# Two tiles in seven products beside one plain tile in the even batches' last chunks, and smaller moves of copies, mends and a bank

## Chip, cores and metric

The kernel runs on one core of one Trainium2 chip. The metric is the time of one execution on the device in microseconds (us).

## The reference

```python
def reference(x, w_tok1, w_tok2, w_ch1, w_ch2):      # x: 8 x 3008 x 256
    X = np.fft.fft(x, axis=1)
    x = np.fft.fft(X, axis=2).real.astype(np.float32)
    xt = x.transpose(0, 2, 1)
    h = np.maximum(xt @ w_tok1, 0.0) @ w_tok2         # 3008 -> 256 -> 3008
    u = x + h.transpose(0, 2, 1)
    h2 = np.maximum(u @ w_ch1, 0.0) @ w_ch2           # 256 -> 1536 -> 256
    return u + h2
```

A Fourier transform over both axes, then a mixing of tokens and a mixing of channels, each with a relu and a residual.

## The kernel before

The program walks 8 batches of 6 chunks. A chunk is up to four tiles of 128 rows. For each of its 12 steps (`ct`) the first channel product `mm1` makes one slice of the hidden layer (`pc` in PSUM, relu into `c1`), while the *previous* chunk's second channel product runs from its finished `c1`. There are two forms of that second product. The plain one (`mm2`) makes a tile with 12 matmuls of 256 columns. The other (`mm2_seven`) takes tiles in pairs and computes 2 x 2 blocks with seven products for eight, each product of 12 matmuls of 128 columns (two pairs), with sums prepared on VectorE. The last chunk of an even batch has only three whole tiles and a half one, so it was done plainly:

```python
    def seven(b, c):                       # which chunks take the seven products
        if c == NCH - 1:
            return b % 2 == 1 and b < BB - 1
        return b > 0 or c >= 2
# [cut]
    def product(dst, left, right, first):
        for a in range(2):                 # two pairs of tiles
            for k in range(NH):            # NH = 6
                nc.tensor.matmul(dst[:, P * a:P * a + P], lhsT=left[:, k, a, :],
                                 rhs=right[:, k, :], start=(first and k + a == 0),
                                 stop=(k == NH - 1), skip_group_check=True)
# [cut]
    sum_at = {0: 1, 1: 2, 3: 4, 4: 3}      # step: sum made on VectorE
    places = {0: 0, 1: -1, 2: 1, 5: 2, 6: 3, 8: 4, 10: 5, 11: 6}   # step: product
# [cut] for b, for c:
            joins = prev is not None and seven(*prev[0:2])
            on_v = ((1, 5, 8), (), ())[c] if b == 0 and c < 3 else () if joins else (0, 3, 6, 9)
            for ct in range(NCT):          # on_v: relus on VectorE, the others on ScalarE
                mm1(b, c, c1, ct, on_v)
# [cut]
                if joins:
                    if ct in places:
                        mm2_seven(*prev, places[ct], pbox)
                    if ct in sum_at:
                        sums(prev[2], pbox, sum_at[ct])
                elif prev is not None and ct % 3 == 2:
                    mm2(*prev, ct // 3, pbox)
# [cut] at the end of a chunk: the half tile is kept for the next batch
            if c == 5 and b % 2 == 0:
                G.tensor_copy(out=tail1[:], in_=c1[:, :, 384:448])
```

Two PSUM banks serve the results: products 0, 2, 4 and 5 gather in one (`pa`), products 1, 3 and 6 in the other (`pb`), and a plain tile with `ks = 2` (`po`) uses that second bank too.

Before the first channel product there is a set-up of 34 us. VectorE folds the input of batch 0 (`fa`, `fb`, `eo`), TensorE transforms it (`pz`), ScalarE copies the result (`z`), TensorE applies the second-stage table `td` (`pw`), and so on through `ph`, `hq`, `pt`, `uv`, `uu`, `pu`, `ut` to the first `pc`. The table needs three small mends on VectorE (and a memset), and these stood in the middle of the fold. Copies of `hp` and `hq` went by turns to VectorE and ScalarE:

```python
    take(fold0, 5)                                   # first half of the fold
    ts(ol[:, 0:1], ol[:, 0:1], 2.0, AT.mult)         # the mends
    ts(td[:, 0:1], td[:, 64:65], 0.5, AT.mult, ol[:, 0:1], AT.add)
    ts(td[:, 65:66], td[:, 64:65], 0.5, AT.mult, ol[:, 0:1], AT.subtract)
    V.memset(td[:, 64:65], 0.0)
    take(fold0, 5)                                   # second half
# [cut]
                copy(g2 % 2, dst[:, 2 * g2:2 * g2 + 2, :].rearrange("p g k -> p (g k)"),
                     ph[:])                          # true: VectorE, false: ScalarE
# [cut]
                pt = ps_f("pt1")
```

## Time and profile before

| | before |
|---|---|
| time, median of 3 runs | 600.62 us (600.14 to 601.08) |
| span in the trace | 598.5 us |
| first `pc` | 34.19 us after the start |
| from first `pc` to the end | 564.3 us |
| TensorE busy | 582.7 us, 97% of the span |

A row of a timeline reads: start in us, duration, engine, line of the program, operation, output <- inputs, sizes, number of instructions joined in the row, and in brackets the idle time of the engine just before with what ended it. Durations of joined rows contain the end of the last instruction. For a rate one takes start to next start.

The split at the first `pc` is the one used throughout: what is before is called set-up, what is after the steady part. A set-up gain is a shorter chain; in the steady part TensorE has hardly any gaps, so a gain there is TensorE time taken away.

### The profile page before, as it was taken

The page shows a single profiled execution, that of the slowest core. Times are in us where ns is not written, and L with a number is a line of the kernel's source. Part 1 is how long each engine was busy: PE and PEld are TensorE (multiplying, and loading weights), DVE is VectorE, ACT ScalarE, POOL GpSimd, SP SyncE. Part 2 cuts the span into 40 slices and gives each one's busy share as a digit, 9 for nine tenths or more (in the row PEclk, how much of TensorE's full clock was granted, in tenths as well). Part 3 has the DMA queues.
Part 4 walks back from the last instruction along what each step waited for, and adds up shares of the span by engine and source line. Part 5 has one row for each costly group of instructions (what it writes and reads, how often), then busy time and mean ns, then how long its engine had stood idle before and what let it go on. Part 6 is the DMA issues. An engine that isn't in the chain of part 4 may idle for free.

```text
span 598.5 us, 15332 instructions
## 1 busy us (share of the span) xinstructions
PE 582.7 (97%) x6273; PEld 418.5 (70%) x6273; DVE 445.2 (74%) x917; ACT 393.9 (66%) x760; POOL 255.3 (43%) x396
## 2 busy tenths in 40 slices
PE   3999999999999999999999999999999999999997
PEld 3756676677767776677767777667776777666776
DVE  8779679675898669766897668856688657966663
ACT  8856764477647865577756866558665876546662
POOL 8650655837554654635348445556555000000000
PEclk9999999999999999999999999999999999999999
DMA  8993912376127814494335632376123422324533
GB/s 155 206 187 72 181 37 60 72 141 109 46 63 133 137 41 69 77 177 54 78 76 100 131 84 55 67 157 104 41 60 79 90 55 55 81 58 78 92 73 88
DMA packets 83415, 55.70 MB, mean 93 GB/s; under 512 B 53778, under 2 KB 80082, under 8 KB 82578
## 3 DMA queue, kind: packets, MB, share of 16 engines
q1 hardware_dynamic: 76816, 36.82, 31.3%
q0 software_dynamic: 6208, 17.63, 16.3%
q8 instruction: 49, 0.80, 0.5%
q10 hardware_dynamic: 320, 0.26, 0.2%
q14 instruction: 22, 0.18, 0.1%
HBM read 35.26 MB, written 24.64 MB: 100 GB/s over the span
## 4 chain that ended last, share of the span: by engine, by line
PE 82%; DVE 1%; issue 0%; DVEq 0%
PE pc L662 35%; PE pa L712 17%; PE pb L712 13%; PE pu L566 6%; PE po L775 4%; PE pt L595 3%; PE py L538 1%; PE pz L471 1%; DVE s L90 1%; PE pw L512 1%; PE pw L508 1%; DVE osb L90 0%; DVE q L90 0%; DVE ut L90 0%; DVE z L101 0%
## 5 line engine op out<-in xcount | busy, mean ns | idle before, releaser
L97 ACT ACTIVATE c<-pc 128x512 f16<-128x512 f32 (+1 forms) x557 | 317.0, 591 | 152.7 <-PE pc L662 135.4
L662 PE MATMUL pc<-ut,wc 128*128 128x512 f16 (+1 forms) x1152 | 316.4, 374 | 0.3 <-DMA wc<-in_moe_w_ch_dram 0.3
L712 PEld LDWEIGHTS <-s 128*128 128x128 f16 x1968 | 123.5, 98 | 37.5 <-DVE s L90 0.6
L662 PEld LDWEIGHTS <-wc 128*128 128x128 f16 x1152 | 97.0, 98 | 50.7 <-issue 3.0
L712 PEld LDWEIGHTS <-c 128*128 128x128 f16 x1476 | 93.0, 97 | 27.8
L90 DVE TENSOR_TENSOR q<-pa,uT 128x256 f32<-128x256 f32 x123 | 52.4, 426 | 48.4 <-PE pa L712 48.3
L90 DVE TENSOR_TENSOR s<-c 128x1536 f16<-128x1536 f16 x82 | 79.3, 968 | 4.7 <-ACT c L97 4.7
L908 POOL COPY hold<-s 128x1 f16<-128x1 f16 x29 | 5.4, 187 | 174.4 <-DVE s L90 174.4
L90 DVE TENSOR_TENSOR osb<-pb,q 128x256 f32<-128x256 f32 x123 | 51.9, 422 | 22.8 <-PE pb L712 19.1
L90 DVE TENSOR_TENSOR ut<-pu,yt 128x512 f16<-128x512 f32 (+1 forms) x96 | 63.2, 671 | 1.2 <-PE pu L566 0.8
L90 POOL TENSOR_TENSOR eo<-sab 96x512 f16<-96x512 f16 x48 | 52.6, 1111 | 1.6
L566 PE MATMUL pu<-w2r,uu 128*128 128x512 f16 (+1 forms) x168 | 50.0, 379 | 0.3 <-DVE ut L90 0.3
L90 POOL TENSOR_TENSOR sab<-fa,fb 96x256 f16<-96x256 f16 (+1 forms) x72 | 46.7, 672 | 0.0
L90 DVE TENSOR_TENSOR s<-s,c 128x1536 f16<-128x1536 f16 x41 | 40.4, 986 | 0.0
L97 ACT ACTIVATE w<-pw 128x257 f16<-128x257 f32 x90 | 34.9, 387 | 8.1 <-PE pw L512 5.2
L90 DVE TENSOR_TENSOR s<-c,s 128x1536 f16<-128x1536 f16 x41 | 39.0, 951 | 0.0
L775 PE MATMUL po<-wc,c 128*128 128x256 f16 x288 | 35.4, 273 | 0.0
L712 PE MATMUL pb<-wc,c 128*128 128x128 f16 x492 | 34.4, 219 | 0.0
L712 PE MATMUL pa<-wc,c 128*128 128x128 f16 x492 | 34.4, 219 | 0.0
L712 PE MATMUL pa<-t2w,s 128*128 128x128 f16 x492 | 34.2, 219 | 0.1
L712 PE MATMUL pb<-t1w,s 128*128 128x128 f16 x492 | 34.2, 219 | 0.0
L712 PE MATMUL pa<-t4w,c 128*128 128x128 f16 x492 | 34.2, 219 | 0.0
(187 smaller groups left out, 728.7 us busy)
## 6 DMA issues: line engine op xcount, KB each, us to landing
out_dram<-osb SPq DMA_DIRECT2D x83, 256.0 KB
xp<-in_x_dram POOLq DMA_DIRECT2D x14, 408.0 KB, 6.3
out_dram<-osb SPq DMA_DIRECT2D x11, 192.0 KB
uT<-ut SPq DMA_TRANSPOSE x96
w2n<-in_moe_w_tok_dram POOLq DMA_DIRECT2D x2, 752.0 KB, 11.2
w1p<-in_moe_w_tok_dram POOLq DMA_DIRECT2D x2, 384.0 KB, 9.0
wc<-in_moe_w_ch_dram POOLq DMA_DIRECT2D x1, 768.0 KB, 14.9
xp<-in_x_dram POOLq DMA_DIRECT2D x2, 272.0 KB, 6.6
```

What stands on the lines that cost most here:

```text
L90: eng.tensor_tensor(out=out_, in0=a, in1=b, op=op)
L97: nc.scalar.activation(out=out_, in_=in_, func=func, scale=scale, **kw)
L471: nc.tensor.matmul(out_, lhsT=rows[:, half * P:half * P + P], rhs=tab, start=True, stop=True)
L508: nc.tensor.matmul(pw[:, 0:256].rearrange("p (h d) -> p h d", h=2)[:, :, 0:65], lhsT=zg[:, 0, g], rhs=td[:, 0:130].rearrange("p (h d) -> p ...
L512: nc.tensor.matmul(pw[:, 64:322].rearrange("p (h d) -> p h d", h=2)[:, :, 0:64], lhsT=zg[:, 1, g], rhs=td[:, 130:258].rearrange("p (h d) - ...
L538: nc.tensor.matmul(py[:, P * k:P * k + P], lhsT=w[:, 4 * c + k, o:o + P], rhs=tab[:, 4 * c + k, :], start=True, stop=True)
L566: nc.tensor.matmul(pu[:, 0:64 * nk], lhsT=uu[:, th, h, :], rhs=w2[:, th, :, 8 * c:8 * c + nk], start=(th == 0), stop=(th == 1))
L595: nc.tensor.matmul(pt[:, o:o + n], lhsT=hw[:, g, c], rhs=w[:, g, w0:w0 + n], start=(g == 0), stop=(g == NG - 1))
L662: nc.tensor.matmul(pc[:, 0:n], lhsT=wc1[:, h, ct * P:(ct + 1) * P], rhs=ut[:, c, h, 0:n], start=(h == 0), stop=(h == 1))
L712: nc.tensor.matmul(dst[:, P * a:P * a + P], lhsT=left[:, k, a, :], rhs=right[:, k, :], start=(first and k + a == 0), stop=(k == NH - 1), s ...
L775: nc.tensor.matmul(po[:, o:o + D], lhsT=c1[:, ct, ks * P:ks * P + P], rhs=wc2[:, ct, 0:D], start=(ct == 0), stop=(ct == NCT - 1))
L908: G.tensor_copy(out=hold[:], in_=pbox[3][:, 0, 0, 0:1])
```

## The change

Its intent is to give the seven products to two of the three tiles in the last chunks of batches 0, 2, 4 and 6 (one pair instead of two), with the third tile done plainly at step 4, and to shorten the set-up:

1. `seven()` is now true for these chunks; `pairs(b, c)` gives 1 for them, and all views of the seven products take that number. When this work joins, all 12 relus of the running chunk go to ScalarE.
2. The copy of the half tile goes from GpSimd at the end of the chunk to VectorE at step 5 of the next.
3. The mends of the table `td` stand behind the whole first fold.
4. One of `hq`'s copies goes from VectorE to ScalarE, and the first `pt` of batch 0 gets another PSUM bank.

```diff
     def seven(b, c):
         if c == NCH - 1:
-            return b % 2 == 1 and b < BB - 1
+            return b < BB - 1
         return b > 0 or c >= 2
+    def pairs(b, c):
+        return 1 if c == NCH - 1 and b % 2 == 0 else 2
+
-    def quads(c1):
-        v = c1[:].rearrange("p c (a i t) -> p c a i t", a=2, i=2)
+    def quads(c1, na):
+        v = c1[:, :, 0:256 * na].rearrange("p c (a i t) -> p c a i t", a=na, i=2)
-    def product(dst, left, right, first):
-        for a in range(2):
+    def product(dst, left, right, first, na):
+        for a in range(na):
# [cut: the same na in sums, halves, mm2_seven; mm2's ends for a tile alone;
#  two generators stepped by hand, same order]
                     if ct in sum_at:
-                        sums(prev[2], pbox, sum_at[ct])
+                        sums(*prev[0:3], pbox, sum_at[ct])
+                    if pairs(*prev[0:2]) == 1:
+                        if ct == 4:
+                            mm2(*prev, 2, pbox)
+                        elif ct == 5:
+                            V.tensor_copy(out=tail1[:], in_=prev[2][:, :, 384:448])
# [cut]
-            if c == 5 and b % 2 == 0:
-                G.tensor_copy(out=tail1[:], in_=c1[:, :, 384:448])
# set-up
-    take(fold0, 5)
+    take(fold0, 10)
     ts(ol[:, 0:1], ol[:, 0:1], 2.0, AT.mult)
     ts(td[:, 0:1], td[:, 64:65], 0.5, AT.mult, ol[:, 0:1], AT.add)
     ts(td[:, 65:66], td[:, 64:65], 0.5, AT.mult, ol[:, 0:1], AT.subtract)
     V.memset(td[:, 64:65], 0.0)
-    take(fold0, 5)
-                copy(g2 % 2, dst[:, 2 * g2:2 * g2 + 2, :].rearrange("p g k -> p (g k)"),
+                copy(g2 in ((1, 3, 5) if dst is hp else (1, 5)),
+                     dst[:, 2 * g2:2 * g2 + 2, :].rearrange("p g k -> p (g k)"),
                      ph[:])
-                pt = ps_f("pt1")
+                pt = ps_f("pt1") if b else ps_mm("pt1")
```

More of the change, by code (lines that the diff above doesn't have):

```diff
@@ L615, in front @@
             yield from rot()
-            yield from y(0)
-            yield from tok1()
+            y0, t1 = y(0), tok1()
+            for piece in (y0, y0, y0, t1, t1):
+                next(piece)
+                yield
             y1 = y(1)
@@ L691, in store, with sums @@
                 in_=osb[64:128, 3, 0:D])
-    def quads(c1):
-        v = c1[:].rearrange("p c (a i t) -> p c a i t", a=2, i=2)
+    def pairs(b, c):
+        return 1 if c == NCH - 1 and b % 2 == 0 else 2
+    def quads(c1, na):
+        v = c1[:, :, 0:256 * na].rearrange("p c (a i t) -> p c a i t", a=na, i=2)
         return (v[:, 0:NH, :, 0], v[:, NH:NCT, :, 0], v[:, 0:NH, :, 1], v[:, NH:NCT, :, 1])
-    def sums(c1, box, k):
-        a11, a12, a21, a22 = quads(c1)
-        box[k] = work.tile([P, NH, 2, P], FP16, tag=f"s{k}", name=f"s{k}", bufs=1)
+    def sums(b, c, c1, box, k):
+        na = pairs(b, c)
+        a11, a12, a21, a22 = quads(c1, na)
+        full = work.tile([P, NH, 2, P], FP16, tag=f"s{k}", name=f"s{k}", bufs=1)
+        box[k] = full[:, :, 0:na]
         if k == 1:
-            tt(box[1][:], a21, a22, AT.add)
+            tt(box[1], a21, a22, AT.add)
         elif k == 2:
-            tt(box[2][:], box[1][:], a11, AT.subtract)
+            tt(box[2], box[1], a11, AT.subtract)
         elif k == 3:
-            tt(box[3][:], a11, a21, AT.subtract)
+            tt(box[3], a11, a21, AT.subtract)
         else:
-            tt(box[4][:], a12, box[2][:], AT.subtract)
-    def product(dst, left, right, first):
-        for a in range(2):
+            tt(box[4], a12, box[2], AT.subtract)
+    def product(dst, left, right, first, na):
+        for a in range(na):
             for k in range(NH):
@@ L714, in product, with halves @@
                                  stop=(k == NH - 1), skip_group_check=True)
-    def halves(ps):
-        return ps[:, 0:2 * P].rearrange("p (a r q) -> p a r q", a=2, q=2)
+    def halves(ps, na):
+        return ps[:, 0:na * P].rearrange("p (a r q) -> p a r q", a=na, q=2)
     def mm2_seven(b, c, c1, uT, k, box):
-        a11, a12, a21, a22 = quads(c1)
-        u = uT[:].rearrange("p (a i) h (q r) -> p (i h) a r q", a=2, q=2)
+        na = pairs(b, c)
+        a11, a12, a21, a22 = quads(c1, na)
+        u = uT[:, 0:2 * na].rearrange("p (a i) h (q r) -> p (i h) a r q", a=na, q=2)
         if k == 0:
             box["a"] = ps_out("pa", 0)
-            product(box["a"], a11, wc2[:, 0:NH, 0:P], True)
+            product(box["a"], a11, wc2[:, 0:NH, 0:P], True, na)
             box["q"] = work.tile([P, 3, 2, 64, 2], FP32, tag="q", name="q", bufs=1)
             box["osb"] = work.tile([P, 4, D + 1], FP32, tag="osb", name="osb", bufs=2)
-        pa, q = halves(box["a"]), box["q"]
-        osb = box["osb"][:].rearrange("p (a i) d -> p i a d", a=2)
+        pa, q = halves(box["a"], na), box["q"][:, :, 0:na]
+        osb = box["osb"][:, 0:2 * na].rearrange("p (a i) d -> p i a d", a=na)
         def lo(i):
@@ L740, in mm2_seven @@
             pb = ps_out("pb", 1)
-            product(pb, a12, wc2[:, NH:NCT, 0:P], True)
-            tt(lo(0), halves(pb), q[:, 0], AT.add)
+            product(pb, a12, wc2[:, NH:NCT, 0:P], True, na)
+            tt(lo(0), halves(pb, na), q[:, 0], AT.add)
         elif k == 2:
-            product(box["a"], box[2], t2w, False)
+            product(box["a"], box[2], t2w, False, na)
             tt(q[:, 1], pa, u[:, 1], AT.add)
@@ L747, in mm2_seven @@
             box["b"] = ps_out("pb", 1)
-            product(box["b"], box[1], t1w, True)
+            product(box["b"], box[1], t1w, True, na)
         elif k == 4:
-            product(box["a"], box[3], t3w, False)
+            product(box["a"], box[3], t3w, False, na)
             tt(q[:, 2], pa, u[:, 3], AT.add)
-            tt(hi(1), halves(box["b"]), q[:, 2], AT.add)
+            tt(hi(1), halves(box["b"], na), q[:, 2], AT.add)
         elif k == 5:
-            product(box["a"], a22, t4w, False)
+            product(box["a"], a22, t4w, False, na)
             tt(lo(1), pa, u[:, 2], AT.add)
         elif k == 6:
-            product(box["b"], box[4], b22, False)
-            tt(hi(0), halves(box["b"]), q[:, 1], AT.add)
-            V.tensor_copy(out=box["osb"][:, :, P:P + 1], in_=box["osb"][:, :, D:D + 1])
+            product(box["b"], box[4], b22, False, na)
+            tt(hi(0), halves(box["b"], na), q[:, 1], AT.add)
+            V.tensor_copy(out=box["osb"][:, 0:2 * na, P:P + 1],
+                          in_=box["osb"][:, 0:2 * na, D:D + 1])
             store(b, c, box["osb"])
@@ L763, in mm2 @@
         last = c == 5
-        if last and b % 2 == 0 and ks == 3:
-            return
+        alone = last and b % 2 == 0
         if ks == 0:
@@ L776, in mm2 @@
                              rhs=wc2[:, ct, 0:D], start=(ct == 0), stop=(ct == NCT - 1))
-        end = ks % 2 == 1 or last and b % 2 == 0 and ks == 2 or fine
+        end = ks % 2 == 1 or alone or fine
         if end:
@@ L801, in mm2 @@
                     in_=osb[64:128, 3, 0:D])
-        elif ks == 3 or last and b % 2 == 0 and ks == 2:
+        elif ks == 3:
             store(b, c, osb)
```

## The prediction

> **What bounds the kernel now.** I read the page of the profile first (busy times, slices), then two wide windows, then the timeline of each engine around the places that the change touches. The page:
>
> ```profile
> PE 582.7 (97%) x6273; PEld 418.5 (70%) x6273; DVE 445.2 (74%) x917; ACT 393.9 (66%) x760; POOL 255.3 (43%) x396
> PE   3999999999999999999999999999999999999997
> PEclk9999999999999999999999999999999999999999
> ```
>
> TensorE is busy in all slices but the first, at full clock; no other engine is over 74%. Busy matmuls may hide waits, so I split the span at 34 us, where the first channel matmuls (pc) start:
>
> ```profile
> 0.00:34.00 34.00, 22.80 (x262) 18.14 (x263) 27.12 (x98) 26.24 (x52) 22.92 (x47) 1.00 1.02 183
> 34.00:598.00 564.00, 559.87 (x6011) 400.36 (x6010) 418.05 (x820) 367.69 (x708) 232.40 (x349) 1.00 0.45 88
> ```
>
> The columns are stretch, length, then busy PE, PEld, DVE, ACT, POOL. Before 34 us TensorE is busy for 22.8 us of 34: set-up is a chain through several engines. After 34 us it misses 4 us of 564. I also took every matmul's start against the next one's: after 34 us only about 1.5 us is lost in visible stalls, all but 0.1 us of it before 183 us. So there are two currencies: after 34 us a gain is **TensorE time removed**, before 34 us it is **chain latency removed**.
>
> **What the Trainium skill says.** "TensorE: Matmul & The Clock Gate", Back-to-back issue gap: about N/2.4 + 2.5 ns warm, so 55.8 ns for 128 columns and 109 for 256. The trace agrees for 128 (0.67 us for 12) and is a little slower for 256 (1.34 us for 12, 111.5 each). The same page's warning that pairs of weight load and matmul sustain 81 ns at N = 128 does not hold here: these products alternate the two and keep 56 ns. "SBUF — State Buffer", Who interferes with whom: VectorE copies in a two-port mode, and its two-input operations in SBUF, exclude GpSimd from a shared port pair for a whole instruction, and the other way round. The trace agrees: the same 4-element copy took 1.21 us inside a GpSimd addition and 0.24 elsewhere:
>
> ```profile
> 108.45 1.21 DVE L759 COPY osb<-osb 128x4 f32<-128x4 f32 x1
> 250.02 0.24 DVE L759 COPY osb<-osb 128x4 f32<-128x4 f32 x1
> ```
>
> **Part 1: the last chunks of the even batches.** These four chunks (batches 0, 2, 4, 6) have three whole tiles and a half one. Before, three plain tiles: 3 x 12 matmuls of 256 columns. After, two tiles as one pair in seven products of 6 matmuls of 128 columns, and one plain tile. The rates come from the timeline of TensorE (start, then duration; I use start to next start):
>
> ```profile
> 256.99 1.50 PE L775 MATMUL po<-wc,c 128*128 128x256 f16 x12
> 258.33 0.59 PE L662 MATMUL pc<-ut,wc 128*128 128x512 f16 x2
> ...
> 260.36 0.84 PE L712 MATMUL pa<-wc,c 128*128 128x128 f16 x12
> 261.03 0.20 PE L496 MATMUL pz<-t1n,pad 96*128 96x24 f16 x2
> ```
>
> A plain tile is 258.33 - 256.99 = 1.34 us; a product of 12 is 261.03 - 260.36 = 0.67, so 6 are 0.335. Before: 3 x 1.34 = 4.02. After: 7 x 0.335 + 1.34 = 3.69. Saved: 0.33 us a chunk, **1.3 us in four**. Seven products for eight save only an eighth of two tiles' 2.68 us, by their nature.
>
> The other engines pay more. ScalarE takes all 12 relus of the chunk in which this work runs, four more than before: 4 x 0.51 = 2.0 us (six in a row took 3.04). It sat idle for about 1.0 to 1.5 us at each group of that chunk in batch 1. VectorE loses those four (4 x 0.68 = 2.7) and the pair's three plain additions (0.82); it gains four half-size sums (0.72 us at 1016 elements and 0.42 at 508, so an estimated 0.56 at 768: 2.2 us), seven additions of 128 columns at 0.29 (2.0), the column copy (0.24) and the tail copy, for which I estimate 0.3 us: 4.7 against 3.5, so +1.2 us in a chunk of some 10.5 us in which its timeline shows four waits of 1 to 1.5 us. Both fit.
>
> What could cost TensorE time is the second output bank: product 1 writes it at step 2, the plain tile at step 4, product 3 at step 6, each after VectorE has emptied it. After the plain tile TensorE has two pc pairs (0.43 each) and product 2 (0.335), so 1.2 us, before it needs the bank; VectorE's three additions took 0.55. That fits with half a microsecond to spare, except in batch 1: there VectorE comes out of batch 0's last chunk with work left and its copies meet GpSimd's addition (108.45 above). I allow 0.4 us of stalls in all, nearly all in batch 1.
>
> **Part 2: the tail copy.** GpSimd loses four copies of 0.83 us and VectorE gains four; nobody waited for them, and the odd chunks that read the result come 50 us later. The new hold before GpSimd's folding delays it by some 2 us in batch 1, but the next chunk's hold was later still. Worth 0.
>
> **Part 3: the mends of the second-stage table.** VectorE, then the engines that follow it:
>
> ```profile
> 13.11 0.14 DVE L84 TENSOR_SCALAR ol<-ol 128x1 f32<-128x1 f32 x1
> 13.35 0.34 DVE L86 TENSOR_SCALAR td<-td,ol 128x1 f16<-128x1 f16 x2
> 13.73 0.72 DVE L90 TENSOR_TENSOR fa<-xp,xm 96x1016 f16<-96x1016 f16 x1
> ...
> 16.31 0.94 PE L476 MATMUL pz<-t1n,eo 96*128 96x96 f16 x11 [0.55 <-DVE eo L90]
> ...
> 17.24 3.13 ACT L97 ACTIVATE z<-pz 128x480 f16<-128x480 f32 x5 [0.28 <-PE pz L476]
> ...
> 20.42 0.23 PE L508 MATMUL pw<-td,z 128*128 128x130 f16 x1 [0.41 <-ACT z L97]
> ```
>
> The mends take 13.73 - 13.11 = 0.62 us in the middle of the fold. Behind it they fall into a pause of 1.09 us that VectorE has before 18.21, and the table is not read before 20.42. So the fold ends 0.6 us sooner and the pz group starts 0.55 sooner. But ScalarE copies z next, and it had waited for only 0.28 us after its previous work; its five copies then run unbroken to 20.37, and TensorE waits for them. So the gain is **0.28 us**, not 0.6.
>
> **Part 4: one copy of hq to ScalarE, and the other bank for pt.**
>
> ```profile
> 29.21 1.28 DVE L101 CAST hq<-ph 128x512 f16<-128x512 f32 x2
> ...
> 29.63 0.72 PE L595 MATMUL pt<-w,hq 128*128 128x127 f16 x10
> 30.54 0.28 PE L595 MATMUL pt<-w,hq 128*128 128x127 f16 x2 [0.19 <-issue]
> ```
>
> VectorE copies hq groups 3 and 5 back to back until 30.49. TensorE runs 10 matmuls (10 x 0.057, so until 30.20), then starts the last two, which need group 5, at 30.54: 0.34 us lost, which the profile puts down to "issue". With group 3 on ScalarE (idle for 0.23 before 28.68 and for 0.55 before 29.83) VectorE is done at about 29.85, before they are needed: **0.34 us**. The other bank for pt keeps the first pt from waiting for a copy that now comes from ScalarE; alone 0. The stepping of the two generators gives the same order as before.
>
> From there the chain is pt, uv and uu on VectorE, pu, ut, pc at 34.19. The profile lays pc's start to a transfer of wc; I take that for a wrong label, because the addition that writes ut runs from 33.45 with two of 0.65 us, the first done at 34.1, and that half of wc was issued at 15.4 to 16.9 with 4.9 us to landing. So all 0.62 us of parts 3 and 4 should reach 34 us. The input of batch 1, for which VectorE waits at 41.97, does not come sooner, but VectorE had pauses of 0.6 us and more after that.
>
> **Sum.** 600.62 - 1.3 - 0.28 - 0.34 + 0.4 = 599.1 us, 0.25% less.
>
> **Rivals.** (a) A new wait on the second output bank, or on VectorE behind GpSimd's port, in all four chunks and not only in batch 1. For: four users of one bank in eight steps, and copies of 1.21 us inside GpSimd's additions. Against: after batch 1 GpSimd has no folding in that part of the chunk (at 250 to 255 us it ends one and issues loads). At 0.5 us a chunk it would eat 2 us: 600.4, no gain. (b) The set-up gain is hidden: pc at 34.19 really waits for wc, or VectorE waits longer for the input of batch 1 and hands that on. Then only part 1 remains: 599.7. (c) More comes of the set-up: stalls between 20 and 30 us (0.75 us beyond the matmuls' own rates) shrink as copies move to ScalarE, and VectorE, freed of relus in four chunks, removes the stalls of batch 1: 598.2. (d) ScalarE becomes the bound in the four chunks with all relus and z copies. Against: the same load already runs in the chunks with seven products, with TensorE at its own rate.
>
> **Range and chances.** The three runs of before spread over 0.94 us. Rival (b) or a bit of (a) sets the upper end, (c) the lower: 598.1 to 600.3. A change of 12 us either way has nothing behind it: the plain matmuls touched are 16 us in all, and only an eighth of two thirds of it can go. Chances: faster 0.005, within 2% 0.99, slower 0.005.
>
> **What would show it.** PE instructions 6273 + 4 x (42 - 24) = 6345, and PE's busy time after 34 us down by about 1.3 us. The pz group starts near 15.75, pw near 20.1, the hq matmuls run unbroken, the first pc near 33.6. In each of the four chunks 12 relus on ScalarE, and no idle TensorE before po or the second pb, except in batch 1. It would be wrong if TensorE waits for osb additions in those chunks at 250, 390 and 530 us, if the first pc stays at 34.2, or if the distance from the first pc to the end does not shrink by about 1 us.

## The result

| | before | changed |
|---|---|---|
| time, median of 4 runs each, same rounds | 600.38 us (600.12 to 601.08) | 598.29 us (597.60 to 598.95) |
| span in the trace | 598.5 us | 595.8 us |
| first `pc` | 34.19 us | 32.91 us |
| from first `pc` to the end | 564.3 us | 562.9 us |
| TensorE busy, matmuls | 582.7 us, 6273 | 581.0 us, 6345 |

The ratio is 0.9963, with a 95% interval of 0.9946 to 0.9981. Ratios here are the mean time of one kernel's runs over that of the other's of the same rounds, so not quite the ratio of the medians quoted. Executions over 1.5% slower than the fastest of the same kernel are left out of the means. The change is in the class "same" at 2%; the time is inside the predicted range, 0.8 us below the predicted value.

The page of the changed kernel, and the window up to 34 us:

```profile
PE 581.0 (98%) x6345; PEld 418.1 (70%) x6345; DVE 452.1 (76%) x940; ACT 403.6 (68%) x777; POOL 262.8 (44%) x393
0.00:34.00 34.00, 23.56 (x268) 18.21 (x269) 26.76 (x98) 26.52 (x53) 23.35 (x47) 1.00 1.03 186
```

The count of matmuls is the predicted 6345. TensorE's busy time fell by 1.7 us, that of VectorE and ScalarE rose by 7 and 10 us without harm to the end. One of the four chunks in the timeline of TensorE (this is work for batch 2's last chunk, at 248 us), with VectorE's additions for the plain tile:

```profile
250.58 0.60 PE L665 MATMUL pc<-ut,wc 128*128 128x512 f16 x2
251.01 1.50 PE L784 MATMUL po<-wc,c 128*128 128x256 f16 x12
252.35 0.38 PE L472 MATMUL pz<-t1n,eo 96*128 96x96 f16 x5
...
252.55 0.56 DVE L90 TENSOR_TENSOR osb<-po,uT 128x128 f32<-128x128 f32 x3 [1.07 <-PE po L784]
253.33 0.59 PE L665 MATMUL pc<-ut,wc 128*128 128x512 f16 x2
253.76 0.50 PE L720 MATMUL pb<-t1w,s 128*128 128x128 f16 x6
254.10 0.38 PE L472 MATMUL pz<-t1n,eo 96*128 96x96 f16 x5
```

The rates held: the plain tile is 252.35 - 251.01 = 1.34 us, product 3 is 254.10 - 253.76 = 0.34 us. No row of TensorE has a bracket: it does not wait for the second bank. The bank is free at about 252.55 + 0.56 = 253.11 and is needed at 253.76.

The set-up:

```profile
13.02 0.69 DVE L90 TENSOR_TENSOR fa<-xp,xm 96x1016 f16<-96x1016 f16 x1
15.52 0.22 PE L477 MATMUL pz<-t1n,eo 96*128 96x96 f16 x1 [0.51 <-DVE eo L90]
16.53 0.34 DVE L86 TENSOR_SCALAR td<-td,ol 128x1 f16<-128x1 f16 x2
16.54 2.85 ACT L97 ACTIVATE z<-pz 128x480 f16<-128x480 f32 x5 [0.28 <-PE pz L477]
19.45 0.23 PE L509 MATMUL pw<-td,z 128*128 128x130 f16 x1 [0.40 <-ACT z L97]
28.70 0.84 PE L596 MATMUL pt<-w,hq 128*128 128x127 f16 x12
32.91 1.46 PE L665 MATMUL pc<-ut,wc 128*128 128x512 f16 x6 [0.31 <-DVE ut L90]
```

The mends (`td`, 16.53) are in VectorE's pause, the second half of the fold starts at 13.02 for 13.73, and the `hq` matmuls run as one group of 12. The first `pc` waits for `ut`, not for a transfer of `wc`, as the prediction had said of the label in the other profile. But `pw` is 0.97 us earlier, not 0.28, and the first `pc` 1.28 us earlier, not 0.62. Two single profiles differ there by more than the parts explain; the experiments had to tell what of it belongs to the change.

### The profile page after: what moved, and what is told of

The parts are those of the page before. It is cut to its first block, busy times and chain, and to the rows that moved or that the text cites. A ratio compares the mean times of both kernels' runs of the same rounds, so it can differ in the third digit from the quotient of the medians.

```text
span 595.8 us, 15511 instructions
## 1 busy us (share of the span) xinstructions
PE 581.0 (98%) x6345; PEld 418.1 (70%) x6345; DVE 452.1 (76%) x940; ACT 403.6 (68%) x777; POOL 262.8 (44%) x393
## 3 DMA queue, kind: packets, MB, share of 16 engines
q1 hardware_dynamic: 76816, 36.82, 32.8%
## 4 chain that ended last, share of the span: by engine, by line
PE 82%; DVE 1%; issue 0%; DVEq 0%
PE pc L665 36%; PE pa L720 18%; PE pb L720 14%; PE pu L567 6%; PE pt L596 3%; PE po L784 2%; PE pz L472 1%; PE py L539 1%; PE pw L513 1%; PE pw L509 1%; DVE s L90 1%; DVE osb L90 0%; DVE ut L90 0%; PE pz L497 0%; DVE q L90 0%
## 5 line engine op out<-in xcount | busy, mean ns | idle before, releaser
L97 ACT ACTIVATE c<-pc 128x512 f16<-128x512 f32 (+1 forms) x573 | 326.8, 591 | 150.1 <-PE pc L665 128.9
L720 PEld LDWEIGHTS <-s 128*128 128x128 f16 x2064 | 130.1, 98 | 41.4 <-DVE s L90 0.9
L720 PEld LDWEIGHTS <-c 128*128 128x128 f16 x1548 | 98.1, 97 | 30.7
L90 DVE TENSOR_TENSOR q<-pa,uT 128x256 f32<-128x256 f32 (+1 forms) x135 | 55.8, 413 | 49.2 <-PE pa L720 48.9
L90 DVE TENSOR_TENSOR s<-c 128x1536 f16<-128x1536 f16 (+1 forms) x90 | 87.2, 968 | 0.4 <-ACT c L97 0.4
L90 DVE TENSOR_TENSOR osb<-pb,q 128x256 f32<-128x256 f32 (+1 forms) x135 | 55.4, 410 | 25.9 <-PE pb L720 22.3
L874 POOL COPY c<-tail 128x768 f16<-128x768 f16 x4 | 3.3, 828 | 114.7 <-ACT c L97 114.7
L90 DVE TENSOR_TENSOR s<-s,c 128x1536 f16<-128x1536 f16 (+1 forms) x45 | 45.0, 999 | 0.0
L90 DVE TENSOR_TENSOR s<-c,s 128x1536 f16<-128x1536 f16 (+1 forms) x45 | 41.5, 921 | 0.0
L90 DVE TENSOR_TENSOR osb<-pa,uT 128x256 f32<-128x256 f32 (+1 forms) x45 | 18.5, 412 | 23.5 <-PE pa L720 23.3
```

The lines of the kernel that those rows point to most:

```text
L90: eng.tensor_tensor(out=out_, in0=a, in1=b, op=op)
L97: nc.scalar.activation(out=out_, in_=in_, func=func, scale=scale, **kw)
```

## The experiments

Theory A: the gain is seven products in the steady part (about 1.1 to 1.3 us) and the rest in the set-up, of which a good part comes from an instruction at the very start that happened to be short in that execution. Theory B: the gain of the set-up is that of the parts themselves, larger than predicted. Rivals for the steady part: waits on the second bank; the tail copy's move mattering after all. Each kernel gave the reference's result.

### 1. Parts 1 and 2 alone

```diff
# before + seven(), pairs(), plain tile at step 4, tail copy on VectorE at step 5
# mends in the middle of the fold, hq copies by turns, pt in its old bank: as before
```

> The kernel before with only the even last chunks in seven products and the tail copy on VectorE; set-up as before. Theory (a third of a microsecond of matmul time per chunk): first pc to the end of the span 562.9 us as in the changed kernel (before: 564.3), first pc where the kernel before has it (34.2, or about 33.9 if the set-up happens to start early), time 1.4 us under before, ratio about 0.9977. Rival (the seven products gain nothing by themselves, a wait eats it, and all comes from set-up): first pc to end 564.3, time as before.

599.16 us (598.74 to 599.93), with before at 600.84 (11 runs in the same rounds): ratio 0.9969 [0.9956, 0.9982]. From the first `pc` to the end it took 563.25 us, 1.1 us less than before. Experiments 2 to 4, without it and in the same set of rounds, took 564.25 to 564.32. This part stands on its own.

Its set-up was slow in another way. Early matmuls in all these traces follow each other at about twice the later spacing (80 ns instead of 42 for 96 columns). The change to the short spacing came at 18.2 us here, and at 10.9 to 14.4 us in every other execution but one that was made to differ (experiment 8). Two successive matmuls of the timeline, still at 80 ns:

```profile
14.36 0.28 PE L476 MATMUL pz<-t1n,eo 96*128 96x96 f16 x1
14.44 0.28 PE L476 MATMUL pz<-t1m,eo 96*128 96x96 f16 x1
```

So its first `pw` (20.87 us) is left out of the comparisons of the set-up below.

### 2 to 4. Parts 3 and 4 together, and each alone

```diff
# 2: parts 3 and 4    3: part 3 alone (take(fold0, 10), mends behind it)
# 4: part 4 alone:
-                copy(g2 % 2, dst[...], ph[:])
+                copy(g2 in ((1, 3, 5) if dst is hp else (1, 5)), dst[...], ph[:])
-                pt = ps_f("pt1")
+                pt = ps_f("pt1") if b else ps_mm("pt1")
```

> The kernel before with only the two set-up parts (mends behind the fold; one hq copy on ScalarE and pt in the other bank). First pc to end 564.3 as before in every theory. Theory A (mends 0.28, hq 0.34, the other 0.66 us of the 1.29 by which the first pc came sooner is a race at 1.9 us between VectorE's index operation and GpSimd that falls out differently from one execution to the next): time 0.6 to 0.8 us under before, ratio about 0.9988, and the first pc at 33.5 or at 32.9, according to whether the index operation took 1.7 or 0.9 us. Theory B (the mends are worth all of it, 0.9 us, and the race nothing): 1.3 us under before, ratio 0.9979, first pc at 32.9 whatever the index operation took.

> The kernel before with only the mends moved. Theory A: first pc 0.28 us sooner where the index operation at 1.9 us took 1.7 us, up to 0.7 where it took 0.9; mean time 0.3 to 0.5 us under before. Theory B: first pc 0.9 us sooner in both, time 0.9 under before. In both the wait of the last two hq matmuls of the first pt stays, 0.34 us.

> The kernel before with only the hq copy on ScalarE and pt in the other bank. Both theories: the 12 hq matmuls of the first pt run unbroken, the distance from the first pw to the first pc falls by 0.34 us from 13.77 to about 13.43; time 0.34 us under before, ratio 0.9994. If the wait only moves (to the relu of uu or to pu): the distance stays 13.8 and so does the time.

| | time, median | ratio | first `pw` | `pw` to first `pc` | `pc` to end |
|---|---|---|---|---|---|
| 2, both | 600.21 | 0.9995 [0.9982, 1.0008] | 19.92 | 13.46 | 564.25 |
| 3, mends | 600.27 | 0.9992 [0.9980, 1.0005] | 19.96 | 13.79 | 564.29 |
| 4, hq | 600.33 | 0.9995 [0.9981, 1.0010] | 20.29 | 13.46 | 564.32 |

(Before in the same rounds: 600.84.) In time none can be told from before. In the traces they can: the hq copy takes 0.31 to 0.33 us from the stretch `pw` to `pc` in experiments 2 and 4, and nothing else there changes. The row of the last two `hq` matmuls, broken off in experiment 3 and part of the group in experiment 4:

```profile
30.09 0.28 PE L595 MATMUL pt<-w,hq 128*128 128x127 f16 x2 [0.19 <-issue]
```

```profile
29.54 0.84 PE L596 MATMUL pt<-w,hq 128*128 128x127 f16 x12
```

The mends give 0.46 us in experiment 3 and 0.50 in experiment 2 against the 20.42 of before. The steady part is that of before in all three, so the set-up's parts bring nothing after the first `pc`, and cost nothing.

### 5. The changed kernel again

> The changed kernel unaltered, as a second look and as the mark for the other three. Theory: pw to pc 13.46 and pc to end 562.9 to 563.3 again, whatever the set-up does; the moment of the first pw varies from 19.4 to about 20.4 with two things that the program does not fix: how long VectorE's index operation at 1.9 us waits (0.95 or 1.72 us in the six profiles so far) and when TensorE's clock warms (matmul spacing halves at 12.3 to 14.4 us in five profiles, at 18.2 in one). Time 2.0 us under before, ratio 0.9965. Rival (set-up is fixed by the program): pw at 19.45 again.

598.88 us (598.64 to 600.00), before at 600.46: ratio 0.9978 [0.9965, 0.9990]; 2.0 us and 0.9965 had been expected. The first `pc` was at 33.65 us, where the first profile had 32.91; `pc` to end 563.31. So the first profile was on the short side in its set-up, and the same program varies there by 0.7 us. Two causes can be seen. The five `z` copies took 3.17 us and not 2.85: three of them, then a wait of 0.19 us for TensorE's `pz`, then two. And the wait of ScalarE for the third of the four `pt` groups was let go late:

```profile
29.75 0.85 PE L596 MATMUL pt<-w,hp 128*128 128x129 f16 x12
30.43 0.83 PE L596 MATMUL pt<-w,hq 128*128 128x127 f16 x12
31.38 0.28 ACT L97 ACTIVATE sp<-pt 128x129 f32<-128x129 f32 x1 [0.34 <-PE pt L596]
```

`sp` reads the result of the first row, which has ended at 30.60. ScalarE was free at 31.04, yet `sp` started at 31.38, just after the *next* group ended at 31.26. That cost 0.34 us of the chain, so `pw` to `pc` was 13.83 here. Of ten executions with part 4 three have such a longer stretch (13.83, 13.80, 13.62), seven are at 13.41 to 13.48. In experiment 7 it is VectorE that starts its `uv` late, by 0.33 us. The program of that stretch is the same in all; what lets a wait go late is not settled.

### 6. The early index operation rewritten

VectorE's index operation at 1.9 us had taken 1.72 us in the profile of before and 0.94 in that of the changed kernel, with no change of the program there. Theory A laid part of the set-up's gain to it. It was rewritten with two tensor inputs and the same result:

```diff
-    ts(ix8[:], ix8f[:], rowi[:], AT.add, 0.0, AT.max)
+    stt(ix8[:], ix8f[:], rowi[:],
+        offrow[:, 2, 0:2 * BB].rearrange("p (b k) -> p b k", k=2), AT.add, AT.max)
```

> The changed kernel with the index operation written as an addition and a maximum against a tile of zeros, so that it is no longer a one-source operation. Theory (that operation waits for GpSimd's load issues and iota because of the shared port): it takes 0.2 to 0.3 us in this and any execution, ScalarE's first m starts at 3.6 to 3.8 instead of 4.5 or 5.2; the first fold stays where the input lands (10.2 to 10.5), so the time gains only 0 to 0.4 us on the changed kernel. Rival (the operation waits for its data, the iota of ix8f): 0.9 or 1.7 us again.

The timeline of VectorE before, then in this experiment:

```profile
1.86 1.72 DVE L86 TENSOR_SCALAR ix<-ix8f,rowi 128x16 int32<-128x16 f32 x1
```

```profile
1.88 0.24 DVE L93 SCALAR_TENSOR_TENSOR ix<-ix8f,rowi,offrow 128x16 int32<-128x16 f32 x1
```

The operation itself is 1.48 us shorter, as the theory of the shared port had it; the rival, that it waits for its data, is refuted, for `ix8f` is still an input. The same holds in experiment 8, whose kernel has the rewritten operation too. The traces fit what it had waited for: a long one ended at 3.58 us, just after GpSimd's index generation ended at 3.55, a short one at 2.81, just after GpSimd's load issue ended at 2.68. ScalarE's first work comes 0.6 us or more sooner, and the time did not move: 598.74 us (598.17 to 600.17), ratio 0.9976 [0.9963, 0.9989] against 0.9978 of experiment 5. `pw` is at 19.82, to the hundredth as in experiment 5. The fold starts at 10.1 to 10.5 us in all traces: after a wait of 0.3 to 0.7 us for its input where the operation is short, and at 10.37 to 10.44 without one where it is long. **Theory A's explanation of the set-up falls for the most part**: the operation's length is not what makes the changed set-up shorter. What it does move is ScalarE's work up to the `z` copies; how much of that reaches the end is taken up below.

### 7. The plain tile one step later

```diff
-                        if ct == 4:
+                        if ct == 5:
                             mm2(*prev, 2, pbox)
-                        elif ct == 5:
+                        elif ct == 7:
                             V.tensor_copy(out=tail1[:], in_=prev[2][:, :, 384:448])
```

> The changed kernel with the plain tile at step 5 instead of 4 (and the tail copy at step 7), so that between the plain tile and the next user of its bank lie one pc pair and at times a pz group (0.43 to 0.65 us) instead of 1.2 to 1.4 us. Theory (the bank is free 0.5 to 0.7 us after the plain tile, so the placing at 4 has room to spare and at 5 has not): TensorE waits 0.1 to 0.4 us before product 3 in each of the four chunks, pc to end grows by 0.4 to 1.2 us to 563.3 to 564.1. Rival (VectorE always empties the bank in time): pc to end 562.9 to 563.0.

600.74 us (600.23 to 601.86): ratio 1.0002 [0.9990, 1.0015]. The whole gain is gone, and `pc` to end is 565.24 us, 2.1 more than with the change. In the timeline, batch 2's last chunk:

```profile
253.70 1.50 PE L784 MATMUL po<-wc,c 128*128 128x256 f16 x12
255.04 0.59 PE L665 MATMUL pc<-ut,wc 128*128 128x512 f16 x2
255.50 0.55 DVE L90 TENSOR_TENSOR osb<-po,uT 128x128 f32<-128x128 f32 x3 [1.31 <-PE po L784]
256.12 0.51 PE L720 MATMUL pb<-t1w,s 128*128 128x128 f16 x6 [0.49 <-DVE osb L90]
```

Two `pc` matmuls take 0.43 us, so product 3 could have started at 255.04 + 0.43 = 255.47. It waited for VectorE's additions and started at 256.12: 0.65 us lost. In the other three chunks 0.38 us is lost, together 1.79 us. The 0.38 is the geometry: `po` ends 1.50 us after its start, the additions take 0.55, a little goes for the hand-over, and product 3 comes 2.15 us after the start of `po` and not 1.77. The further 0.27 here is VectorE starting at 255.50, 0.30 after the end of `po` at 255.20, where it starts 0.04 us after it in the other three; again a wait let go late. A further 0.84 us was lost at 131 us, where before and the changed kernel lose 0.2 to 0.5.

This is rival (a) of the prediction made true on purpose, and it costs what that rival said. It also measures the slack of the chosen place: at step 4 product 3 comes 253.76 - 251.01 = 2.75 us after the start of `po` where 2.15 would do, 0.6 us in this chunk; of this 0.21 are `pz` matmuls, which batch 0's chunk does not have there.

### 8. The clock warmed early

```diff
+    warm = const.tile([P, P], FP16, tag="warm", name="warm")
+    V.memset(warm[:], 1.0)
     def filler(n):
         pw = ps_out("filler", 0)
+        for _ in range(64 if n > 4 else 0):
+            nc.tensor.matmul(pw[:, 0:P], lhsT=warm[:], rhs=warm[:], start=True, stop=True)
# and the index operation of experiment 6
```

> The kernel of the start_free run with 64 more filler matmuls at the very start, on a tile of ones, so that TensorE is busy from about 1 us. Theory (when the clock warms is a matter of TensorE's activity, and a late one costs set-up time): spacing is warm by 5 to 8 us, the set-up's first group of pt transposes and pz runs at full clock, first pc at 32.3 to 32.8 in every execution, time 0.2 to 0.6 us under the changed kernel on the mean. Rival (the fold alone sets the pace, the clock is hidden): no change against start_free.

If the time of the step to the short spacing (18.2 us in experiment 1) mattered, fillers from 1 us on should gain. They ran:

```profile
1.06 5.79 PE L402 MATMUL filler<-warm 128*128 128x128 f16 x64 [1.06 <-DVE warm L176]
```

The short spacing came at 5.41 us, 4.35 us after the first filler. The Trainium skill ("TensorE: Matmul & The Clock Gate", Part 1: The HAM clock gate) says that the clock is let up after around 4 us of sustained matmuls, by a window that runs free of the program; the 4.35 us agree. The other executions, whose early matmuls are broken by pauses, scatter by 3.5 us. The time was 599.40 us (598.38 to 602.08), ratio 0.9988 [0.9973, 1.0003] against 0.9976 of experiment 6, whose kernel has all but the fillers. `pw` came at 19.86 and the first `pc` at 33.48, not at 32.3 to 32.8: no gain. The set-up's early matmuls have enough slack to run at the slow spacing. Whether the late step of experiment 1 is what made its `pw` late was not tested.

### 9. The tail copy back on GpSimd, at its new place

```diff
                         elif ct == 5:
-                            V.tensor_copy(out=tail1[:], in_=prev[2][:, :, 384:448])
+                            G.tensor_copy(out=tail1[:], in_=prev[2][:, :, 384:448])
```

> The changed kernel with the tail copy back on GpSimd, at the same step 5. Theory (part 2 is worth nothing, since nobody waits for the tail): pc to end 562.9 to 563.3 as in the changed kernel, time within 0.5 us of it. Rival (the copy belongs on VectorE for a reason: on GpSimd it delays the folding and shares the port with VectorE's sums): pc to end longer by 0.3 us or more.

599.72 us (598.27 to 599.84), ratio 0.9987 [0.9974, 1.0001]; before at 600.14. The interval does not tell it from the changed kernel. `pc` to end is 563.61 us, longer than in the changed kernel by the 0.3 us or more that the rival had named. TensorE lost 0.84 us in batch 1, where the changed kernel lost 0.07:

```profile
107.17 1.21 DVE L768 COPY osb<-osb 128x4 f32<-128x4 f32 x1
108.29 1.22 POOL L898 COPY tail<-c 128x768 f16<-128x768 f16 x1
110.18 1.05 PE L784 MATMUL po<-wc,c 128*128 128x256 f16 x8 [0.68 <-DVE osb L90]
```

In the changed kernel's first profile the same four-element copy took 0.19 us:

```profile
107.29 0.19 DVE L768 COPY osb<-osb 128x4 f32<-128x4 f32 x1
```

So VectorE came late to empty the bank for `po`. A sum behind the copy took 0.97 us, but 1.22 in the changed kernel, so it is not what was lost. The copy starts 0.15 to 0.17 us before the first of two GpSimd additions of the fold (`eo`) ends, in all 14 profiles. With the tail copy on GpSimd it waits out the second addition (1.20 to 1.21 us in six of six: before twice, experiments 2, 3, 4 and 9); with the tail copy on VectorE it goes through (0.18 to 0.19 in eight of eight). So the long copy follows the program and not chance, and by this profile part 2 is worth some 0.8 us in batch 1, where I had predicted 0. The tail copy itself only starts after the second addition; how its place decides between the two is open.

### 10. `pt` in its old bank

```diff
-                pt = ps_f("pt1") if b else ps_mm("pt1")
+                pt = ps_f("pt1")
```

> The changed kernel with the first pt of each half back in the bank group that it had before. Theory (the other bank group is worth nothing by itself): pw to pc 13.4 to 13.5, or 13.8 in an execution in which a wait on TensorE is released late as in the second look; hq matmuls unbroken. Rival (without the move, pt waits for one of the other users of its bank group): a visible pause of TensorE before the second pt or before the hq matmuls, pw to pc 13.7 or more.

599.56 us (598.55 to 600.18), ratio 0.9985 [0.9972, 0.9999]. The local question has an answer: `pw` to `pc` is 13.41 us and the `hq` matmuls are unbroken, so the new bank is not what gains. `pc` to end was 564.98, for another reason. Batch 1's input came 2 us later in this execution than in the changed kernel's (VectorE started its fold at 43.86 and not at 41.73), and TensorE waited for `ut`, 1.59 us from start to start:

```profile
53.03 0.38 PE L665 MATMUL pc<-ut,wc 128*128 128x512 f16 x1 [1.43 <-DVE ut L90]
```

That is the mechanism of rival (b), a late input of batch 1 handed on to TensorE. It was seen in this execution and, with 0.11 us at 51.7 us, in experiment 11. In the changed kernel's own two profiles it was not. A second loss of both, 0.67 us at 72.7 and 71.4 us, is of another kind: `ut` stood behind a sum of VectorE that took 2.46 and 2.45 us beside GpSimd's copies, where the other profiles looked at have 1.90 to 2.03. Whether the old bank has a part in it is open; the input's arrival doesn't depend on that bank in any way that I can see.

### 11. The last `z` copies of two batches on ScalarE

The changed kernel still loses up to 0.45 us at 131 us, where TensorE waits for a copy of `z` on VectorE. This gave that group to ScalarE from batch 2 on:

```diff
-            copy(half, zo, pz[:, 0:96].rearrange("p (u k) -> p u k", u=4))
+            copy(half and b < 2, zo, pz[:, 0:96].rearrange("p (u k) -> p u k", u=4))
```

> The changed kernel with VectorE's copy of the second pad group of z moved to ScalarE from batch 2 on. TensorE waits for that copy at 131 us for 0.17 to 0.45 us in every profile, more in the kernels with the seven products. Theory (VectorE is behind there with its sums): that wait goes and nothing else changes, pc to end 562.5 to 562.9, time 0.3 us under the changed kernel. Rival (the copy waits for the same late release of TensorE's semaphore on ScalarE too, or ScalarE is now late with the relus): no gain.

The wait at 131 us in experiment 5, then here, in the timeline of TensorE:

```profile
131.60 0.23 PE L513 MATMUL pw<-td,z 128*128 128x128 f16 x1 [0.29 <-DVE z L101]
```

```profile
131.42 0.23 PE L513 MATMUL pw<-td,z 128*128 128x128 f16 x1
```

The matmul ahead of it started at 131.09 there and at 131.24 here, so start to start went from 0.51 to 0.18 us. With 0.06 us for the matmul itself the loss went from 0.45 to 0.12 us. That is not all the edit's: experiments 9 and 10, without it and in the same set of rounds as 11, lost only 0.17. The theory of 0.3 us is not borne out. `pc` to end is 563.38, not 562.5 to 562.9, with the loss at 71.4 us in it; the time is 598.33 us (598.01 to 599.77), ratio 0.9976 [0.9962, 0.9991], not to be told from the changed kernel's. No experiment gave a version that is clearly faster.

### 12. The kernel before, a second profile

> The kernel before, unaltered, for a second look at its set-up. Expected: pw to pc 13.77, pc to end 564.3; first pw between 20.3 and 20.9. If the 1.29 us between the first profiles was all the program's, the first pc comes at 34.2 again; if 0.3 to 0.5 of it was the luck of one execution, anywhere from 33.9 to 34.6.

600.00 us. First `pw` 19.99 and first `pc` 33.77 us where the first profile had 20.42 and 34.19; `pw` to `pc` 13.78, `pc` to end 564.22. Both marks lie below what was expected (20.3 to 20.9 and 33.9 to 34.6). So before, too, varies by 0.4 us in its set-up, and the first pair of profiles compared a long set-up of before with a short one of after. ScalarE in this profile:

```profile
17.08 2.86 ACT L97 ACTIVATE z<-pz 128x480 f16<-128x480 f32 x5 [0.84 <-PE pz L476]
```

It waited 0.84 us for the fold's result, where the first profile said 0.28. This is the row that the mis-sized term of the prediction rests on.

## Why the prediction was right, and where a term was off

The time was predicted as 599.1 us and came out at 598.29 and 598.88 in the two sets of rounds. All the mechanisms named in the sum are there. One gain was too small and one loss too large, which lie on the same side; part 2 was misjudged; and 0.25 us of the gain lie outside the span, where the prediction had not looked.

**Part 1, right in its working.** `pc` to end has a mean of 564.28 us in the five profiles whose steady part is that of before (564.22 to 564.32) and of 563.15 in the five with the seven products that run it undisturbed (562.93 to 563.31: the changed kernel twice, experiments 1, 6 and 8). That is 1.13 us less, and the scatter is small. Left out are the four with an edit in that part or a disturbance in it (7, 9, 10, 11); experiment 10, the steady part unedited but batch 1's input late, would make the second mean 563.45 and the difference 0.83. The 1.3 us of TensorE time are confirmed by the rates. The 0.4 us of new stalls were too many: about 0.1 to 0.2 us of the 1.3 is missing in the difference. What changed is small both ways. Before's two waits of 0.11 us ahead of plain tiles, at 116.8 and 540 us, are gone; new is 0.07 us ahead of `po` in batch 1, the one place that the prediction named; and the `z` wait at 131 us went from a mean of 0.24 us (0.17 to 0.29, five profiles) to 0.37 (0.17 to 0.45, five). New too is a wait of 0.06 to 0.22 us ahead of a product at 398 us in four of those five. The prediction had put nearly all of its 0.4 us in batch 1, because a copy of VectorE met GpSimd's addition there; in the changed kernel it no longer does (experiment 9). The estimates for VectorE's pieces held: a half-size sum takes 0.55 us (estimated 0.56), the tail copy 0.34 to 0.35 in three chunks (estimated 0.3), and 1.04 in batch 1, beside GpSimd. In all VectorE's busy time rose by 6.9 us, where 4 x 1.2 = 4.8 had been worked out. ScalarE has 16 relus more.

**Rival (a), refuted for this place, and closer than it was told.** The prediction gave half a microsecond to spare after the plain tile. Experiment 7 shows that moving it by one step makes a wait of 0.38 to 0.65 us in each chunk, and no gain is left. The prediction had left the end of the last matmul (1.50 against 1.34) and the hand-over out of that slack.

**Part 3, the mis-sized term.** The prediction said: "So the gain is **0.28 us**, not 0.6", from the 0.28 us that ScalarE had waited ahead of its `z` copies. The kind of step is sound: `z` starts when the later of two things is there, the fold's result through `pz` or a free ScalarE. Its size failed twice over. First, it was read from one profile, in which ScalarE happened to be late. Executions in which the early clock was slow (experiment 1) or the start was altered (6, 8) are left out; 7, 10 and 11 read like the last rows of their kind:

| execution | index operation | ScalarE idle before `z` | `z` starts | first `pw` |
|---|---|---|---|---|
| before, first profile | 1.72 | 0.28 | 17.24 | 20.42 |
| before, second profile (12) | 0.95 | 0.84 | 17.08 | 19.99 |
| hq alone (4) | 0.96 | 0.87 | 17.07 | 20.29 |
| changed, first profile | 0.94 | 0.28 | 16.54 | 19.45 |
| tail copy on GpSimd (9) | 0.95 | 0.32 | 16.44 | 19.34 |
| changed, second profile (5) | 0.95 | none shown | 16.59 | 19.82 |
| mends alone (3) | 1.72 | none shown | 16.74 | 19.96 |
| set-up parts alone (2) | 1.72 | none shown | 16.73 | 19.92 |

Where the index operation at 1.9 us took 1.72 us, ScalarE's work was some 0.75 us later (its `m` started at 5.24 us and not at 4.49 us). With a short one ScalarE had 0.84 us to spare in the old order, and the fold's 0.55 us come through whole: 17.08 to 16.54, with 0.28 us still idle. Second, where it was long the gain was still not 0.28 but 0.5 us (17.24 to 16.74 and 16.73). The row of experiment 2, in which ScalarE does not wait:

```profile
16.73 3.13 ACT L97 ACTIVATE z<-pz 128x480 f16<-128x480 f32 x5
```

The copies ahead of it are a row of 1.59 us that started at 15.30, so by durations they end at 16.89, and `z` starts 0.16 us before that. A queued instruction of ScalarE starts before the duration of the one ahead of it has run out. An idle time counted from end to start is therefore too small as a slack: in the first profile it was 0.28 + 0.16 = 0.44 us. The prediction used start to next start for TensorE and should have done so for ScalarE. That is worked out from rows, and agrees with the 0.5; no experiment isolates it.

This is also how far the index operation reaches: with the mends moved, `z` starts at 16.44 to 16.66 with a short one and at 16.73 to 16.78 with a long one, some 0.2 us. Theory A had wanted most of the set-up's gain from it. The mean of the first `pw` is 20.23 us in the three executions without the move (before twice, and 4) and 19.74 in the ten with it (19.34 to 19.96): **0.49 us in place of 0.28**. The last digit is not sure, with three against ten.

What looks like luck in single profiles has a pattern. In before's first profile and in experiments 2 to 8 one of the five `z` copies starts 0.25 to 0.31 us late, behind a wait for TensorE's `pz`, and the five take 3.13 to 3.18 us; in the changed kernel's first profile and in 9 to 12 none does, and they take 2.85 to 2.89. The wait at 131 us splits in the same way: 0.23 us or more in before's first profile and in experiments 1 to 8, 0.17 in the others (0.12 in 11, whose code there is altered). Experiments 1 to 8 ran on chips 7 and 10, and 9 to 12 on chip 6, so this may go with the chip or the set of rounds; no run separates them. The first pair compared the two kinds, and about 0.28 of its 0.97 us is that. Within each kind the mends are worth the same: the first `pw` goes from 20.36 to 19.89 us (two and six profiles) and from 19.99 to 19.52 (one and four), **0.47 us** both times.

**Part 4, right.** Predicted 0.34 us. The stretch `pw` to `pc` is 13.78 us in the mean of four without it; it is 0.29 to 0.36 us shorter in the seven executions in which nothing is let go late, and 0.23 in the mean of ten with the three late ones in it. The bank alone is worth nothing, as predicted.

**Rival (b), not in force, but real.** The steady part didn't lose what the set-up gained. The late input of batch 1 that the rival had in mind was seen in experiment 10, and as a trace of 0.11 us in 11.

**Rival (c), in part.** The set-up gave more than 0.62 us. In two profiles of before's set-up the first `pc` has a mean of 33.98 us; in seven of the changed set-up (the changed kernel twice, experiments 2, 7, 9, 10, 11) 33.24: 0.74 us less. The other half of the first pair's 1.28 us is not the change's: a `z` copy let go late in one and not in the other, and an index operation that was long in one and short in the other. It did not come through stalls between 20 and 30 us, which that rival named.

**The sum.** 1.13 + 0.74 = 1.87 us within the span. The time of an execution is also longer than its span, by 1.92 to 2.14 us in all executions of kernels without the seven products in the even last chunks and by 1.72 to 1.87 in all with them (experiment 1 included). These 0.25 us are part of the gain, the prediction has no term for them, and no experiment tells their cause. Together that is 2.12 us, where the medians of the two sets say 2.09 and 1.58, and the prediction said 1.5. So theory B holds in its main point: the set-up's gain is that of its two parts, 0.49 + 0.23 = 0.72 us (but not the 0.9 us that it gave the mends), and what the first pair of profiles showed beyond it was not the change's.

**Part 2, wrong.** "Worth 0" rested on nobody waiting for the copy, which holds. What failed is the step from there: with the copy on GpSimd, VectorE's four-element copy waits out GpSimd's addition in batch 1, and TensorE loses 0.84 us instead of 0.07 (experiment 9). The time that this costs is seen in one profile of that kernel, the long copy in all six without the move. Why the place of a later GpSimd instruction decides it is open.

## What to carry to other kernels

When a gain is capped by another engine's idle time, read that idle time from more than one profile, and from start to start: here it was 0.28 us in one execution and 0.84 in the next of the same program, and it set the size of the gain. Compare profiles of the same set of rounds, and look for a row that sorts them before calling a difference luck. When TensorE is busy for 99% of a stage, the gain there is the matmul time taken away, and it can be worked out beforehand to 0.2 us; but check each shared bank from the *end* of the last matmul that writes it, for one step in the order can cost the whole gain. And compare a stage between marks within the trace (here the first `pc` to the end, which scatters by 0.1 to 0.4 us), when the times of whole executions scatter by more than the gain.

## What the Trainium skill lacked or had wrong

- "TensorE: Matmul & The Clock Gate", Back-to-back issue gap: it gives about 81 ns at 128 columns and 131 ns at 512 as what a stream of pairs of weight load and matmul sustains. Here products of 128 columns, each matmul with its own weight load, keep 56 ns (0.67 us for 12), and the `pc` matmuls of 512 columns 216 ns (0.43 us for two). The page's formula for single matmuls fits this kernel. Plain tiles of 256 columns took 111.5 ns against 109 by the formula; the cause was not tested.
- Same page, Part 1: The HAM clock gate: right on the start (5.41 us with fillers from 1.06 us on; 10.9 to 14.4 us without, once 18.2). It does not say that the early slow stretch can be hidden: 64 fillers gained nothing (ratio 0.9988 against 0.9976 without them).
- "SBUF — State Buffer", Who interferes with whom: it agrees with the copies of 1.21 us in place of 0.19 to 0.25 beside GpSimd, and with the index operation, of a kind (`tensor_scalar`) that it lists among those that can take the shared pair: 0.95 or 1.72 us beside GpSimd, 0.24 rewritten as an operation of another kind. It says that whichever issues first blocks the other; by the recorded starts that does not sort the profiles of experiment 9. There the four-element copy starts 0.11 to 0.13 us ahead of a GpSimd addition in all 14, but waits it out in six of six with one kind of program (1.20 to 1.21 us) and goes through in eight of eight with the other (0.18 to 0.19).
- Of the pages drawn on here none has this: a wait on TensorE's results let go 0.27 to 0.34 us late, at the end of a later group of matmuls, in some executions of an unchanged program (experiments 5 and 7), and one of 0.25 to 0.31 us ahead of a `z` copy in eight of thirteen profiles. The cause is open.
